# Matmuls of constants in the gaps of TensorE during the first batch's attention

## The chip, the cores and the metric

The kernel runs on one core of one Trainium2 chip. The metric is the device time of one execution in microseconds (us). It was measured three times: 954.39, 951.01 and 953.71 us, median 953.71. One more execution was recorded by the hardware profiler; its page and trace are read below.

The engines are named as in the profile: PE is TensorE's matmul part, PEld its weight loads, DVE VectorE, ACT ScalarE, POOL GpSimd, and SP the engine that issues the DMAs. L182 is line 182 of the kernel before.

## What is computed

A sparse attention with 8 heads over a batch of 8 sequences of 576 positions, and behind it a mixing step over positions and a feed-forward network:

```
scores = (q @ k.T) / sqrt(64)
mask_local   = (rel >= 0) & (rel < 32)                 # heads 0 to 3
mask_strided = (rel >= 0) & (key % 32 == query % 32)   # heads 4 to 7
attn = softmax(where(mask, scores, -1e9))
x = (attn @ v), heads side by side                     # 8 x 576 x 512
h = x.T @ U @ V                                        # 576 -> 32 -> 576, over positions
u = x + h.T
out = u + relu(u @ w_ch1) @ w_ch2                      # 512 -> 2048 -> 512
```

U, V and both weight matrices are 64-bit floats in memory.

## The kernel before

**Stages.** The work has a prefix and nine blocks of 512 positions. The prefix is the attention of batch 0 (`first_attention`, L495), its mixing step, and the first conversions of weights. The nine blocks (the loop at L600) are the two matmuls of the feed-forward network, L431 and L449, each done as three products of high and low parts so that the result has nearly full precision. Into the blocks the loop works the attention and mixing of the next batch.

**The prefix.** Batch 0 has four pairs of heads, in the order 0, 2, 3, 1, started three steps apart (`run_staggered`). One pair goes through this chain:

- `scores` (L140): two bf16 matmuls put the mask into the accumulator (L143), then 36 small f32 matmuls add the scores of 32 queries and up to 64 keys each (L149). In the trace an f32 matmul is two passes, each with its weight load, so a pair's scores are 72 matmul and 72 load records, and 4 for the mask.
- `probabilities` (L154): maximum and subtraction on DVE (L157, L158), exponential on ACT (L161).
- `transposed` (L167): five transpositions on PE (L171), a copy on ACT (L174): 10 records on PE, 5 matmuls and 5 loads.
- `outputs` (L177): 36 small f32 matmuls with the values (L182), 144 records.
- `normalised` (L187): DVE writes the result to `x_loc` or `x_str`.

After the four pairs follow the mixing step (`mix_t`, L319 and L323, and its casts L332 and L333 on ACT), transpositions of the batch's data (L386), the products with V (L359), and then the first matmuls L431 of block 0.

**Weights.** `convert` makes 32-bit floats, split into a high and a low part, out of 32 chunks of 64-bit weights: ACT (L84), DVE (L86, L87, L89), ACT (L112), POOL (L113). The loads of all chunks (`raw`, 512 KB each) are issued on SP right behind the inputs of the attention, so that the queues are full through the prefix. `gate` orders a conversion on ACT behind the last exponential or mixing step.

**What sets the order.** A scheduler reorders the program with a time model of its own (`schedule_with_timeline_sim`), and each engine then runs its own list in order. `tc.issue_after(x)` only tells that scheduler that an instruction is to stand behind `x`. PE's accumulators: `ph` (two buffers) belongs to the first matmul of the network, `acc` and `px` are used by turns in the prefix (`psx2`).

Of the kernel before, what the change touches and what calls it, by code (L numbers as in the profile page):

```python
# [7 lines left out]
F32 = mybir.dt.float32  # L8
F32R = mybir.dt.float32r
BF16 = mybir.dt.bfloat16  # L10
# [6 lines left out]
B, H, S, D = 8, 8, 576, 64  # L17
# [6 lines left out]
NB = B * S // TB  # L24
NSP = 2
LAG = 2
STAGGER = 3
ATT_BUFS = 7
PAIR_ORDER = (0, 2, 3, 1)
# [4 lines left out]
def fused_kernel(ctx, tc, lqk, lv, eqk, ev, sqkv, U, V, wts, masks, eye, out):  # L34
    nc = tc.nc
    const = ctx.enter_context(tc.tile_pool(name="const", bufs=1))
# [5 lines left out]
    ps_h = ctx.enter_context(tc.tile_pool(name="ps_h", bufs=2, space=bass.MemoryType.PSUM))  # L42
    ps_x = ctx.enter_context(tc.tile_pool(name="ps_x", bufs=1, space=bass.MemoryType.PSUM))

    def att(shape, name, dtype=F32):
        return ap_.tile(shape, dtype, name=name, tag="att", bufs=ATT_BUFS)

    banks = {"n": 0, "prefix": True}

    def psx2():  # L50
        banks["n"] += 1
        if banks["prefix"] and banks["n"] % 3:
            return ps_acc.tile([128, 2, 512], F32, name="acc")
        return ps_x.tile([128, 2, 512], F32, name="px")

    last_dma, gate, exps = [None], [], []

    def dma(out, in_):
        last_dma[0] = nc.sync.dma_start(out=out, in_=in_).ins
# [15 lines left out]
    def wtag(i, g, t):  # L75
        return f"w{i}_{g}_{t}"

    def to_f32(raw, p, n, paced=False, after=None):
        rv = raw.bitcast(I32).rearrange("p (n two) -> p n two", two=2)
        lo_w, hi_w = rv[:, 0:n, 0], rv[:, 0:n, 1]  # L80
        cv = att([128, 576], "cv")
        f = cv[0:p, 0:n]
        with tc.issue_after(gate[0]) if paced and gate else nullcontext(), tc.issue_after(after) if after else nullcontext():
            nc.scalar.activation(out=f, in_=hi_w.bitcast(F32), func=AF.Abs, scale=2.0 ** -112)  # L84
        i = cv.bitcast(I32)[0:p, 0:n]
        nc.vector.tensor_scalar(out=i, in0=i, scalar1=3, scalar2=None, op0=ALU.logical_shift_left)  # L86
        nc.vector.scalar_tensor_tensor(out=i, in0=hi_w, scalar=-0x80000000, in1=i,  # L87
                                       op0=ALU.bitwise_and, op1=ALU.bitwise_or)
        nc.vector.scalar_tensor_tensor(out=i, in0=lo_w, scalar=29, in1=i,  # L89
                                       op0=ALU.logical_shift_right, op1=ALU.bitwise_or)  # L90
        return f
# [3 lines left out]
    def load_weights(n):  # L95
        while wl["loaded"] < min(n, len(chunks)):
            k = wl["loaded"]
            c = chunks[k]
            raws[c] = const.tile([128, 512], I64, name="raw%d_%d_%d" % c, tag=wtag(*c))
            with tc.issue_after(last_dma[0]):  # L100
                dma(out=raws[c], in_=wts[k])
            wl["loaded"] += 1

    def convert(n):
        while wl["conv"] < min(n, len(chunks)):
            k = wl["conv"]
            load_weights(k + 1)
            c = chunks[k]
            f = to_f32(raws[c], 128, 512, True, halves_done[-2] if len(halves_done) > 1 else None)
            parts = const.tile([128, 2, 512], F32R, name="w%d_%d_%d" % c, tag=wtag(*c))  # L110
            w_parts[c] = parts
            halves_done.append(nc.scalar.copy(out=parts[:, 0], in_=f).ins)  # L112
            nc.gpsimd.tensor_tensor(out=parts[:, 1], in0=f, in1=parts[:, 0].bitcast(F32), op=ALU.subtract)  # L113
            wl["conv"] += 1
# [7 lines left out]
    def small_loads():  # L122
        dma(out=raw_u, in_=U)
        dma(out=raw_v, in_=V)
# [15 lines left out]
    def scores(kT, qT, mask):  # L140
        sp = psx2()
        for hh in range(2):
            nc.tensor.matmul(sp[:, hh, 0:320], ident_b, mask, start=True, stop=False, skip_group_check=True)  # L143
        for c in range(NCH):
            t, c4 = c // 4, c % 4
            k0 = max(0, 32 * c - 32)
            x0 = 64 * t + (0 if c else 32)
            for hh, rows in enumerate(halves):
                nc.tensor.matmul(sp[32 * c4:32 * c4 + 32, hh, x0:64 * t + 64], qT[rows, 32 * c:32 * c + 32],  # L149
                                 kT[rows, k0:32 * c + 32], start=False, stop=True, skip_group_check=True,  # L150
                                 tile_position=(64 * hh, 32 * c4))
        return sp[:, :, 0:320].rearrange("p h (t x) -> p h t x", x=64)

    def probabilities(sp):  # L154
# [12 lines left out]
    def transposed(s_sb):  # L167
        pp = psx2().rearrange("p a x -> p (a x)")
        for t in range(5):
            n = 128 if t < 4 else 64  # L170
            nc.tensor.transpose(out=pp[:, 128 * t:128 * t + n], in_=s_sb[0:n, t].rearrange("p h x -> p (h x)"),  # L171
                                identity=ident[0:n, 0:n])
        PT = att([128, S], "PT")
        nc.scalar.copy(out=PT, in_=pp[:, 0:S])  # L174
        return PT

    def outputs(PT, vt):  # L177
        op = psx2()
        for c in range(NCH):
            t, c4 = c // 4, c % 4  # L180
            for hh, rows in enumerate(halves):
                nc.tensor.matmul(op[32 * c4:32 * c4 + 32, hh, (D + 1) * t:(D + 1) * t + D + 1], PT[rows, 32 * c:32 * c + 32],  # L182
                                 vt(c)[rows], start=True, stop=True, skip_group_check=True,
                                 tile_position=(64 * hh, 32 * c4))
        return op[:, :, 0:5 * (D + 1)].rearrange("p h (t x) -> p h t x", x=D + 1)

    def normalised(op, pr):  # L187
# [32 lines left out]
    def attention_pair(b, pr, loaded=None):  # L220
# [9 lines left out]
        yield  # L230
        PT = transposed(s_sb)
        yield
        yield
        op = outputs(PT, vt)
        yield
# [122 lines left out]
    def mixed(ps, b, dc, V, s0, s1, start):  # L358
        nc.tensor.matmul(ps, tsts[b][:, 128 * dc:128 * dc + 128], V[:, s0:s1], start=start, stop=True,  # L359
                         skip_group_check=True)  # L360

    def u_local(b, dcs):
        px = psx2()
        for dc in dcs:
            ps = px[:, dc % 2]
            for t in range(4):
                nc.tensor.matmul(ps[:, 128 * t:128 * t + 128], x_loc[:, t, 128 * dc:128 * dc + 128], ident,  # L367
                                 is_transpose=True, start=t == 0, stop=False, skip_group_check=True)
            mixed(ps, b, dc, Vst, 0, TB, False)
        lo, hi = dcs[0] % 2, dcs[-1] % 2 + 1  # L370
        split(b, slice(dcs[0], dcs[-1] + 1), px[:, lo:hi], nc.vector)
# [123 lines left out]
    def first_attention():  # L495
        scratch = [up.tile([128, NDC * TB], F32, name="scr", tag=t) for t in ("uh", "ul")]
        late = [const.tile([128, 9, D + 1], F32, name=f"ve{n}", tag=wtag(n // 4, 3, n % 4)) for n in range(8)]
        loads = {}

        def load(k):  # L500
            pr = PAIR_ORDER[k]
            if k < 3:
                qk = [scratch[j // 3][:, S * (j % 3):S * (j % 3) + S] for j in (2 * k, 2 * k + 1)]
            else:
                qk = [att([128, S], "kT"), att([128, S], "qT")]
            loads[k] = pair_loads(0, pr, (*qk, late[2 * k], late[2 * k + 1]))

        load(0)
        dma(out=masks_sb, in_=masks)
        dma(out=ident, in_=eye)  # L510
        load(1)
        load(2)
        small_loads()
        load(3)
        load_weights(24)
        nc.gpsimd.memset(x_loc[64:128, 4], 0.0)
        nc.gpsimd.memset(x_str[64:128, 4], 0.0)
        pairs = [attention_pair(0, pr, loads[k]) for k, pr in enumerate(PAIR_ORDER)]
        beside = {3: lambda: (small_u(), small_v()), 4: lambda: convert(2)}
        seen = 0  # L520
        steps = run_staggered(pairs, STAGGER)

        def go(n):
            nonlocal seen
            for _ in range(n):
                if next(steps, "end") == "end":
                    return
                if len(exps) > seen:
                    seen = len(exps)
                    beside.get(seen, lambda: None)()  # L530

        go(3 * STAGGER + 8)
        mix_t(0, 1)
        go(2)
        u_strided_early(0, 2)
        go(40)
        mix_t(0, 0)
        u_strided_early(0, 3)
        for dc in range(2):
            u_local(0, (dc,))  # L540
        convert(5)

    first_attention()
# [56 lines left out]
    for n in range(NB):  # L600
        tasks, t = plan(n), 0
        done.clear()
        for fc in range(NFC):
            if n == 0:
                convert(needed(fc))
            gens = [gemm1(n, fc)]
            if len(pend) >= LAG:
                gens.append(gemm2(*pend.pop(0)))
# [91 lines left out]
```

## Time and profile before

| What | Value |
| --- | --- |
| median of 3 timed runs | 953.71 us (951.01 to 954.39) |
| the profiled execution | 954.11 us |
| its span, first to last instruction | 952.3 us |
| PE busy | 917.1 us, 96% of the span |
| DVE, POOL, ACT busy | 536.9, 403.4, 247.3 us |
| moved by DMA | 64.50 MB, mean 68 GB/s |

The page gives averages over the whole span. What matters here is the first 160 us, so the views below are the timeline and the windows of that stretch. In a row of the timeline stand start, duration, engine, line, operation, output and inputs, the count, and in brackets the idle time of the engine just before it with what ended it; "issue" stands for a wait that nothing in the profile explains. The granted clock is the share of TensorE's full speed that its throttle lets through.

### The profile page before, as it was taken

Reading aid. Unit: us, or ns where it says so; the run is one execution under the profiler, and the core shown is the slowest. Engines: PE = TensorE matmul, PEld = TensorE weight load, DVE = VectorE, ACT = ScalarE, POOL = GpSimd, SP = SyncE. Lnnn points to the kernel's source line nnn. Section 1 sums busy time; section 2 is a strip of 40 time slices with the busy share of each in tenths; the row PEclk is TensorE's granted clock in tenths of the full one; section 3 lists DMA queues with packets and bytes.
Section 4 is the critical chain, followed back from the end, with each engine's and each line's share of the span. In section 5 each row is a group of like instructions: output and inputs, shape, how many; then the busy total and the mean of one; then the engine's idle time right before and its main releaser. Section 6 shows DMA issues by size and latency. Waiting matters only on the chain.

```text
span 952.3 us, 16503 instructions
## 1 busy us (share of the span) xinstructions
PE 917.1 (96%) x6896; PEld 725.8 (76%) x6896; DVE 536.9 (56%) x912; ACT 247.3 (26%) x486; POOL 403.4 (42%) x407
## 2 busy tenths in 40 slices
PE   5789898999999999999999999999999999999998
PEld 3557566878787787778778878787778788888886
DVE  4686778548936693659465964597448831112112
ACT  2443345212421142114311341115112521111110
POOL 0142233565639471939185816763575530002000
PEclk9989998999999999999999999999999999999999
DMA  9962202111022101220122003110210020001001
GB/s 338 408 259 67 77 27 75 45 57 52 25 79 71 52 26 56 70 76 5 41 105 77 1 25 119 33 51 26 95 56 26 1 80 15 1 1 45 1 1 44
DMA packets 27098, 64.50 MB, mean 68 GB/s; under 512 B 6768, under 2 KB 7280, under 8 KB 27024
## 3 DMA queue, kind: packets, MB, share of 16 engines
q1 hardware_dynamic: 27024, 63.45, 19.2%
q8 instruction: 54, 0.88, 0.4%
q14 instruction: 20, 0.16, 0.1%
HBM read 52.96 MB, written 10.49 MB: 67 GB/s over the span
## 4 chain that ended last, share of the span: by engine, by line
PE 79%; issue 9%; DVE 4%; POOL 3%; DMA 3%; ACT 0%; SPq 0%; POOLq 0%; DVEq 0%
PE ph L431 37%; PE acc L449 36%; POOL w L113 3%; DVE st L289 2%; DMA raw<-in_wts_dram 2%; PE px L182 1%; PE px L149 1%; PE px L359 1%; PE px L171 1%; DMA ve<-in_ev_dram 1%; PE px L319 1%; PE acc L462 1%; PE px L367 1%; DMA masks_sb<-in_masks_dram 0%; DVE ta L328 0%
## 5 line engine op out<-in xcount | busy, mean ns | idle before, releaser
L431 PE MATMUL ph<-uh,w 128*128 128x512 f32 x1152 | 393.3, 401 | 10.1 <-ACT w L112 5.1
L449 PE MATMUL acc<-gh,w 128*128 128x512 f32 x1136 | 375.4, 392 | 2.2 <-ACT gh L437 1.5
L431 PEld LDWEIGHTS ph<-uh,w 128*128 128x128 f32 x1152 | 217.9, 191 | 62.0 <-ACT w L112 6.7
L449 PEld LDWEIGHTS acc<-gh,w 128*128 128x128 f32 x1136 | 212.7, 188 | 49.0 <-ACT gh L437 2.3
L438 DVE SCALAR_TENSOR_TENSOR gl<-ph,gh 128x512 fp32r<-128x512 f32 x144 | 99.0, 689 | 239.6 <-ACT gh L437 239.0
L431 PE MATMUL ph<-ul,w 128*128 128x512 f32 x576 | 228.7, 398 | 0.0
L449 PE MATMUL acc<-gl,w 128*128 128x512 f32 x568 | 222.4, 392 | 0.0
L261 POOL TENSOR_TENSOR tmp<-st 128x576 f32<-128x576 f32 (+6 forms) x162 | 166.2, 1070 | 88.5 <-DMA st<-in_sqkv_dram 45.4
L437 ACT ACTIVATE gh<-ph 128x512 fp32r<-128x512 f32 x144 | 85.7, 597 | 365.2 <-PE ph L431 341.3
L287 POOL TENSOR_TENSOR tmp<-st,s_st 128x448 f32<-128x448 f32 (+7 forms) x162 | 135.5, 875 | 59.1 <-DVE s_st L280 59.1
L289 DVE TENSOR_REDUCE st<-tmp 128x64 f32<-128x64 f32 (+8 forms) x162 | 133.6, 882 | 1.2 <-POOL tmp L287 0.9
L431 PEld LDWEIGHTS ph<-ul,w 128*128 128x128 f32 x576 | 109.9, 191 | 23.5 <-DVE ul L351 0.6
L449 PEld LDWEIGHTS acc<-gl,w 128*128 128x128 f32 x568 | 106.8, 188 | 22.9 <-issue 0.4
L263 DVE TENSOR_REDUCE s_st<-tmp 128x9 f32<-128x576 f32 (+6 forms) x162 | 87.9, 566 | 44.3 <-POOL tmp L261 44.1
L113 POOL TENSOR_TENSOR w<-cv,w 128x512 fp32r<-128x512 f32 x32 | 43.6, 1369 | 99.2 <-ACT w L112 92.7
L479 POOL TENSOR_TENSOR o<-o,uh 128x512 f32<-128x512 f32 x32 | 40.7, 1297 | 92.8 <-DVE o L478 92.8
L351 POOL TENSOR_TENSOR ul<-st,uh 128x1024 fp32r<-128x1024 f32 x6 | 14.4, 2399 | 103.4 <-ACT uh L350 103.4
L304 ACT COPY x_str<-st 32x256 f32<-32x256 f32 x96 | 38.8, 404 | 36.2 <-DVE st L289 35.0
L87 DVE SCALAR_TENSOR_TENSOR cv<-raw,cv 128x512 int32<-128x512 int32 x32 | 28.4, 892 | 0.4
L112 ACT CAST w<-cv 128x512 fp32r<-128x512 f32 x32 | 19.7, 620 | 31.2 <-DVE cv L89 26.4
L89 DVE SCALAR_TENSOR_TENSOR cv<-raw,cv 128x512 int32<-128x512 int32 x32 | 27.4, 862 | 0.4
L161 ACT ACTIVATE s_sb<-s_sb 128x640 f32<-128x640 f32 x20 | 14.8, 740 | 49.2 <-DVE s_sb L158 49.1
(117 smaller groups left out, 504.4 us busy)
## 6 DMA issues: line engine op xcount, KB each, us to landing
raw<-in_wts_dram SPq DMA_DIRECT2D x32, 512.0 KB, 10.2
st<-in_sqkv_dram SPq DMA_DIRECT2D x18, 576.0 KB, 4.9
out_dram<-o SPq DMA_DIRECT2D x35, 256.0 KB, 2.0
vt<-in_lv_dram SPq DMA_DIRECT2D x14, 585.0 KB, 3.8
kT<-in_lqk_dram SPq DMA_DIRECT2D x15, 288.0 KB, 2.7
qT<-in_lqk_dram SPq DMA_DIRECT2D x15, 288.0 KB, 3.1
ve<-in_lv_dram SPq DMA_DIRECT2D x4, 292.5 KB, 6.0
ve<-in_ev_dram SPq DMA_DIRECT2D x4, 292.5 KB, 5.5
```

Of the source, the lines that this page charges most:

```text
L87: nc.vector.scalar_tensor_tensor(out=i, in0=hi_w, scalar=-0x80000000, in1=i, op0=ALU.bitwise_and, op1=ALU.bitwise_or)
L113: nc.gpsimd.tensor_tensor(out=parts[:, 1], in0=f, in1=parts[:, 0].bitcast(F32), op=ALU.subtract)
L261: nc.gpsimd.tensor_tensor(out=tmp[:, 0:n], in0=sk[:, j0:j0 + n], in1=sq[:, i:i + 1].broadcast_to([128, n, D]), op=ALU.mult)
L263: late.append(lambda tmp=tmp, n=n, i=i, j0=j0: nc.vector.tensor_reduce(out=s_st[:, i, j0:j0 + n], in_=tmp[:, 0:n], axis=AX.X, op=ALU.add))
L287: nc.gpsimd.tensor_tensor(out=tv, in0=sv[:, 0:i + 1, d0:d0 + step], in1=s_st[:, i, 0:i + 1].broadcast_to([128, i + 1, step]), op=ALU.mult)
L289: late.append(lambda tv=tv, i=i, d0=d0, step=step: nc.vector.tensor_reduce(out=sq[:, i, d0:d0 + step], in_=tv.rearrange("p j d -> p d j"), ...
L304: nc.scalar.copy(out=xh[32 * i4:32 * i4 + 32, 0:4], in_=oh[:, i4:16:4])
L431: nc.tensor.matmul(ph, w_parts[0, g, dc][:, part, fs], ut[:, dc, :], start=(k == 0 and i == 0), stop=(k == NDC - 1 and i == 2))
L437: gate[:] = [nc.scalar.activation(out=gh, in_=ph, func=AF.Relu).ins]
L438: nc.vector.scalar_tensor_tensor(out=gl, in0=ph, scalar=0.0, in1=gh.bitcast(F32), op0=ALU.max, op1=ALU.subtract)
L449: nc.tensor.matmul(accs[n][m // 2][:, m % 2], w_parts[1, g, f][:, part, ms], gt, start=(fc == 0 and i == 0), stop=(fc == NFC - 1 and i == 2))
L479: nc.gpsimd.tensor_tensor(out=o, in0=o, in1=uh[:, m].bitcast(F32), op=ALU.add)
```

## The change

A constant tile `warm_w` (128 x 128, bf16, all ones) is made by a memset on POOL. `fill` issues matmuls of that tile with itself into a `ph` buffer; nobody reads the results. There are 80 at the very start, and 20 for each of twelve spots: the last matmul of `scores`, `transposed` and `outputs` of each of the four pairs. The fills of the spots are issued in the program behind `u_local` and ahead of the last conversions, each to stand behind its spot; the scheduler chooses where.

```
+FIRST_FILL, FILL = 80, 20
...
+    warm_w = const.tile([128, 128], BF16, name="warm_w")
+    spots = []
+
+    def spot(matmul):
+        if banks["prefix"]:
+            spots.append(matmul.ins)
+
+    def fill(after, n):
+        ps = ps_h.tile([128, 512], F32, name="ph")
+        for _ in range(n):
+            with tc.issue_after(after) if after is not None else nullcontext():
+                nc.tensor.matmul(ps[:, 0:128], warm_w, warm_w[:, 0:128], start=True, stop=True)
...
# in scores, transposed and outputs: the last matmul of the loop is kept
-                nc.tensor.matmul(sp[...], ...)
+                m = nc.tensor.matmul(sp[...], ...)
+        spot(m)
...
# in first_attention
+        nc.gpsimd.memset(warm_w, 1.0)
+        fill(None, FIRST_FILL)
         load(0)
         dma(out=masks_sb, in_=masks)
...
         for dc in range(2):
             u_local(0, (dc,))
+        for m in spots:
+            fill(m, FILL)
         convert(5)
```

On PE the scheduler put the 240 fills of the spots into seven runs: 26 behind the second scores, 34 behind the first transposition, 34 behind the second, 69 behind the third, 42 behind the fourth, 35 behind the first mixing step and its transposition; together 240. The order of the other matmuls of the prefix stays as it was. In the changed kernel the lines have other numbers: scores are L156 and L162, transpositions L185, outputs L197, the mixing step L335 and L339, its transposition L402, a fill L69.

The first place is PE between the second scores and the first outputs. Before (`s_sb` holds the probabilities, `PT` their transposition, `ve` the values):

```order
L143 MATMUL acc<-masks_sb 128x320
L149 MATMUL acc<-scr 32x32 x2
L149 MATMUL acc<-scr 32x64 x34
L171 MATMUL px<-ident,s_sb 128x128 x4
L171 MATMUL px<-ident,s_sb 128x64
L182 MATMUL acc<-ve_90,PT 32x65 x18
L182 MATMUL acc<-ve_91,PT 32x65 x18
```

The same place of the changed kernel, from the last of the 26 fills to the first of the 34 (each fill is a weight load and a matmul):

```order
L69 LDWEIGHTS warm_w
L69 MATMUL ph<-warm_w 128x128
L185 MATMUL px<-ident,s_sb 128x128 x4
L185 MATMUL px<-ident,s_sb 128x64
L69 LDWEIGHTS warm_w
L69 MATMUL ph<-warm_w 128x128
```

The transposition now stands between two runs of fills, with 52 instructions ahead of it and 68 behind it that were not there.

The second place is PE from the last outputs to the mixing step (`x_str` and `x_loc` are the attention's results, `U_sb` is U). Before:

```order
L182 MATMUL px<-ve_96,PT 32x65 x18
L182 MATMUL px<-ve_97,PT 32x65 x18
L319 MATMUL acc<-x_str,U_sb 32x256 x4
L323 MATMUL acc<-x_str,U_sb 32x64 x4
L386 MATMUL acc<-ident,x_str 128x128 x4
L386 MATMUL acc<-ident,x_str 128x64
L319 MATMUL px<-x_loc,U_sb 32x256 x4
```

In the changed kernel, from the last of the 42 fills to the first of the 35:

```order
L69 MATMUL ph<-warm_w 128x128
L197 MATMUL px<-ve_97,PT 32x65 x18
L197 MATMUL px<-ve_98,PT 32x65 x18
L335 MATMUL acc<-x_str,U_sb 32x256 x4
L339 MATMUL acc<-x_str,U_sb 32x64 x4
L402 MATMUL acc<-ident,x_str 128x128 x4
L402 MATMUL acc<-ident,x_str 128x64
L69 LDWEIGHTS warm_w
L69 MATMUL ph<-warm_w 128x128
```

84 instructions stand ahead of the last outputs, and 70 between the two halves of the mixing step. On DVE and ACT a few neighbours change places, and in block 0 some matmuls of L449 stand earlier against those of L431; POOL has the one memset more, ahead of all others, and SP's list is the same.

More of the change, by code (lines that the diff above doesn't have):

```diff
@@ L148, in scores @@
             for hh, rows in enumerate(halves):
-                nc.tensor.matmul(sp[32 * c4:32 * c4 + 32, hh, x0:64 * t + 64], qT[rows, 32 * c:32 * c + 32],
+                m = nc.tensor.matmul(sp[32 * c4:32 * c4 + 32, hh, x0:64 * t + 64], qT[rows, 32 * c:32 * c + 32],
                                  kT[rows, k0:32 * c + 32], start=False, stop=True, skip_group_check=True,
                                  tile_position=(64 * hh, 32 * c4))
+        spot(m)
         return sp[:, :, 0:320].rearrange("p h (t x) -> p h t x", x=64)
@@ L170, in transposed @@
             n = 128 if t < 4 else 64
-            nc.tensor.transpose(out=pp[:, 128 * t:128 * t + n], in_=s_sb[0:n, t].rearrange("p h x -> p (h x)"),
+            m = nc.tensor.transpose(out=pp[:, 128 * t:128 * t + n], in_=s_sb[0:n, t].rearrange("p h x -> p (h x)"),
                                 identity=ident[0:n, 0:n])
+        spot(m)
         PT = att([128, S], "PT")
@@ L181, in outputs @@
             for hh, rows in enumerate(halves):
-                nc.tensor.matmul(op[32 * c4:32 * c4 + 32, hh, (D + 1) * t:(D + 1) * t + D + 1], PT[rows, 32 * c:32 * c + 32],
+                m = nc.tensor.matmul(op[32 * c4:32 * c4 + 32, hh, (D + 1) * t:(D + 1) * t + D + 1], PT[rows, 32 * c:32 * c + 32],
                                  vt(c)[rows], start=True, stop=True, skip_group_check=True,
                                  tile_position=(64 * hh, 32 * c4))
+        spot(m)
         return op[:, :, 0:5 * (D + 1)].rearrange("p h (t x) -> p h t x", x=D + 1)
```

## The prediction

> **What bounds the kernel now.** I read the page first, then the idle time by stage, then the PE timeline of the stage that the change touches.
>
> ```profile
> PE 917.1 (96%) x6896; PEld 725.8 (76%) x6896; DVE 536.9 (56%) x912; ACT 247.3 (26%) x486; POOL 403.4 (42%) x407
> q8 instruction: 54, 0.88, 0.4%
> 7.39:41.77 34.38, 26.39 (x650) 17.33 (x650) 21.55 (x55) 12.14 (x21) 4.07 (x3) 1.00 1.03 398
> 46.90:60.00 13.10, 8.90 (x34) 5.44 (x33) 12.90 (x18) 7.29 (x14) 5.39 (x4) 0.89 1.03 409
> 160.00:952.30 792.30, 787.43 (x5273) 632.60 (x5272) 428.03 (x710) 181.52 (x371) 361.43 (x370) 1.00 0.14 45
> ```
>
> The second row is PE's instruction queue: packets, MB, share. The last three rows are windows: stretch, length, busy time of PE, PEld, DVE, ACT and POOL, granted clock, DMA share, GB/s. From 160 us on PE is busy 787.43 of 792.30 us, and the change adds nothing there: what it does is decided by when the dense part can begin. Between the first scores at 7.39 and the first dense matmul at 41.77 PE is idle for 34.38 - 26.39 = 7.99 us, and all 16 DMA engines are full (1.03, 398 GB/s of weights and inputs).
>
> Which wait ends last there? The timeline, with PE's own pauses in brackets:
>
> ```profile
> 9.93 1.31 PE L149 MATMUL acc<-scr 64*32 64x32 f32 x72
> 15.31 0.18 PEld L182 LDWEIGHTS acc<-ve,PT 64*32 64x32 f32 x3 [0.21 <-issue]
> 21.75 0.43 PEld L182 LDWEIGHTS acc<-ve,PT 64*32 64x32 f32 x28 [1.35 <-issue]
> 21.75 0.68 PE L182 MATMUL acc<-ve,PT 64*32 64x65 f32 x28 [1.11 <-issue]
> 22.35 0.13 PEld L143 LDWEIGHTS <-masks_sb 128*128 128x128 bf16 x2 [0.17 <-DVE cv L89]
> 22.36 0.72 PE L143 MATMUL acc<-masks_sb 128*128 128x320 bf16 x2
> 23.00 1.07 PEld L149 LDWEIGHTS acc<-kT,qT 64*32 64x32 f32 x72 [0.52 <-issue]
> 23.00 1.31 PE L149 MATMUL acc<-kT,qT 64*32 64x32 f32 x72
> 24.24 0.71 PEld L171 LDWEIGHTS px<-ident,s_sb 128*128 128x128 f32 x4 [0.17 <-issue]
> 24.24 1.41 PE L171 MATMUL px<-ident,s_sb 128*128 128x128 f32 x5
> 25.28 0.18 PEld L171 LDWEIGHTS px<-ident,s_sb 64*128 64x128 f32 x1 [0.33 <-issue]
> 26.43 0.40 PEld L182 LDWEIGHTS acc<-ve,PT 64*32 64x32 f32 x20 [0.97 <-ACT PT L174]
> 26.43 0.64 PE L182 MATMUL acc<-ve,PT 64*32 64x65 f32 x19 [0.78 <-ACT PT L174]
> 28.12 1.10 PE L182 MATMUL acc<-ve,PT 64*32 64x65 f32 x53 [1.05 <-issue]
> 34.32 0.42 PE L182 MATMUL px<-ve,PT 64*32 64x65 f32 x3 [0.40 <-issue]
> ```
>
> PE stops for "issue", that is for no engine, in the middle of four of its output batches (L182): at 15.31, 21.75, 28.12 and 34.32. The steps are 6.44, 6.37 and 6.20 us, on average 6.34. Count the instructions from 21.75 to 28.12: 28+28, 2+2, 72+72, 5+5, 20+19 loads and matmuls make 253. The page's instruction queue q8 moved 54 packets (0.88 MB) for 2 x 6896 PE instructions, 255 to a packet. So each pause falls where one packet of PE's program ends and the next has to be there. The DMA view of 19.10 to 21.75, and of the quiet stretches on both sides of 41.4, has the packets:
>
> ```profile
> q1 hardware_dynamic: 291, 1.06, 100.4%
> q8 instruction: 1, 0.02, 2.5%
> ...
> q14 instruction: 1, 0.01, 0.3%
> ...
> q8 instruction: 1, 0.02, 2.7%
> ```
>
> One q8 packet comes just before the pause at 21.75 ends. Between 34.33 and 41.40 there is none (q14 belongs to another engine), and the next comes in 41.40 to 44.00: up to 7 us after the block at 34.32 began. So I read this stage as **bound by the fetch of PE's instructions**: beside full data queues a new block of some 255 instructions is there every 6.34 us at best, and a faster PE would only wait longer.
>
> A skill rule stands against this: the Trainium skill, "Runtime: NRT & Kernel Launch", Instruction fetch mechanics, says that the program comes in blocks of 256 instructions and that the cost of a block's border is mostly hidden. The trace agrees on the block and not on the cost. By the rule the added instructions would cost only their own time, which is the first rival below.
>
> **The change, part by part.** It adds 320 bf16 matmuls of 128x128, each with its weight load: 640 PE instructions, 80 pairs ahead of the first scores and 240 in seven runs (26, 34, 34, 69, 42, 35; and 80 makes the first). Nothing is removed. POOL gets one memset first. For one pair the trace has no row; the nearest are these:
>
> ```profile
> 0.73 0.31 POOL L516 MEMSET x_loc<- 64x256 f32 x1 [0.29 <-POOLq L688]
> 43.49 1.05 PE L431 MATMUL ph<-uh,w 128*128 128x512 f32 x2
> 44.34 0.63 PE L431 MATMUL ph<-ul,w 128*128 128x512 f32 x1
> 66.45 0.61 PE L431 MATMUL ph<-uh,w 128*128 128x512 f32 x2
> 66.90 0.39 PE L431 MATMUL ph<-ul,w 128*128 128x512 f32 x1
> 7.39 0.13 PEld L143 LDWEIGHTS <-masks_sb 128*128 128x128 bf16 x2 [7.39 <-DMA masks_sb<-in_masks_dram]
> ```
>
> Two dense matmuls of 512 columns take 0.85 us at 43.49 (slow PE) and 0.45 us at 66.45 (fast PE), so 128 columns take 0.107 or 0.057 us. The load, 0.13 / 2 = 0.065, lies beside the matmul before it; were it in the way, a pair would take up to 0.17. I take 0.107 and 0.057, since the dense stream is the like case. **The first 80 pairs** start at about 1.05 (0.73 and a memset like x_loc's 0.31) and last 4.6 to 8.6 us: they end between 5.6 and 9.7. The masks land at 7.39, so I let the scores begin at 8.0.
>
> **The fetch** is the large term. Count instructions from the first score: a pair's scores are 148, a transposition 10, an output batch 144. Before, blocks began at counts 445, 696, 949 and 1203, all inside outputs. The borders stay near these counts, but the new program has 160 fills first, and more between. In it count 445 lies at the end of the second scores, 700 in the first outputs, 953 at the second, 1207 in the fourth scores, 1460 in the third outputs and 1714 in the fourth: **six block starts where there were four**. The border at 189 stood in the second scores (row 9.93) at about 10.2, and the block at 445 came 15.31 - 10.2 = 5.1 us later. Now count 189 is in the first scores, at about 8.2; so 445 comes at 13.4, and five steps later, at 13.4 + 5 x 6.34 = 45.1, the last part of the fourth outputs can run. What follows it before the first dense matmul is seen here:
>
> ```profile
> 34.68 1.08 PE L319 MATMUL acc<-x_str,U_sb 128*32 128x256 f32 x8
> 41.77 1.22 PE L431 MATMUL ph<-uh,w 128*128 128x512 f32 x2 [0.48 <-ACT uh L350]
> ```
>
> From 34.68 to 41.77 is 7.1 us; to it come 0.6 for the 66 instructions left of the outputs and 2.8 for the run of 35 fills (between 35 x 0.057 = 2.0 and 35 x 0.107 = 3.7), and 0.7 goes if PE is fast half of the time. The first dense matmul then starts at 45.1 + 0.6 + 7.1 + 2.8 - 0.7 = 54.9, not at 41.77: **13.1 us later**.
>
> The other fills (205 in the gaps) I cost at nothing, because the fetch covers them: where PE is fast, a block with its fills has at most some 5.6 us of work against 6.34. If PE is slow that cover is gone (the second rival).
>
> **Is it made good later?** The rows that carry the delay on:
>
> ```profile
> 45.64 0.40 ACT L333 CAST tst<-ta 32x256 fp32r<-32x256 f32 x1
> 46.06 1.24 ACT L84 ACTIVATE cv<-raw 128x512 f32<-128x512 f32 x2
> 50.13 0.73 PE L431 MATMUL ph<-uh,w 128*128 128x512 f32 x2 [1.45 <-ACT w L112]
> 57.10:64.00 6.90, 5.82 (x14) 4.62 (x15) 6.70 (x10) 2.70 (x5) 2.97 (x2) 0.51 0.79 297
> ```
>
> The next weight conversion (L84) follows the casts of the mixing step (L333) on ACT, and PE waits for converted weights at 50.13; DVE is busy 12.90 of 13.10 us from 46.90. ACT, DVE, POOL and SP keep their work in nearly the same order, so this stage moves as a whole and I carry all of the 13.1 us. A fast PE in 41.77 to 46.90 would reach the same wait for weights sooner: nothing. The slow spell at 57.10 to 64.00 (granted clock 0.51) follows idle time; if it doesn't return, up to 2.9 us of PE's 5.82 are won, and if there is one more as much is lost. I take zero.
>
> Sum against the profiled execution: 954.11 (span 952.3 and 1.8 around it) + 13.1 = 967.2. The median of the three timed runs is 953.71, 0.4 lower; I say **967.0**.
>
> **The rivals.** *1. A fast PE, and the fetch hides: not slower.* For it: PE was slow throughout this stage, as like operations show, early and late:
>
> ```profile
> L171 PE MATMUL px<-ident,s_sb 128*128 128x128 f32 x12 | 3.3, 434 | 0.7 <-ACT s_sb L161 0.7
> L182 PE MATMUL acc<-ve,PT 64*32 64x65 f32 x216 | 5.1, 312 | 4.4 <-ACT PT L174 2.2 <-issue 2.2
> ...
> L171 PE MATMUL px<-ident,s_sb 128*128 128x128 f32 x12 | 1.9, 277 | 1.0 <-ACT s_sb L161 1.0
> L182 PE MATMUL px<-vt,PT 64*32 64x65 f32 x216 | 2.9, 225 | 0.8 <-ACT PT L174 0.8
> ```
>
> 434 against 277 ns and 312 against 225: about 0.3 of the 26.39 us, 8 us, could go. (The granted clock of 1.00 in that window can't be the whole record, since like operations take a third less later; the durations decide.) With the 7.99 idle that is room for 16, and the 240 fills take 240 x 0.057 = 13.7: 2 us earlier at best, 951.5. The Trainium skill, "TensorE: Matmul & The Clock Gate", Part 1, speaks for this rival: PE runs at half clock until some 3.4 us of steady matmuls, and falls back after a like idle window. The trace agrees with it in 57.10 to 64.00: in the 13.10 us from 46.90 PE was idle for 4.2. Against the rival: the four pauses. The point: solving 13.4 + 5s + 9.8 = 41.77 gives s = 3.7; if a block comes every 3.7 us or faster, the change isn't slower.
>
> *2. The fills don't keep PE fast: it does not do what it says.* The pauses leave PE without work for microseconds, and it may fall back each time. Then blocks overrun the fetch: the block of S2's end, 26 and 34 fills, transposes and outputs takes 8.7 us (+2.4), that with 69 fills 9.6 (+3.3), the other two about 0.7 each, the last run of 35 0.9 more, the lost 0.7, and a start at 9.6 in place of 8.0: some 10 us, at 977.
>
> *3. The fetch is quicker than 6.34,* as the first 5.1 us step was: 5 x 1.2 = 6 less, 961.
>
> **How the numbers follow.** Forecast 0.60, first rival 0.12, second 0.15, third 0.13. The range takes the forecast, the third with 2.9 us for the lost slow spell (961 - 3 = 958) and the second (977, and one late packet as after 34.32): 958 to 978. A measurement of this kernel can tell about 0.5% (4.8 us) from no change. Faster by more than that would need over twice the best that the first rival has: 0.03; same 0.12 with the milder end of the third; slower 0.85.
>
> **What would show it.** Right: "issue" pauses of PE 250 to 256 instructions apart, about 6.3 us from one to the next, six of them and some within scores; the first dense matmul near 55; the dense stage after it as long as before. The fills at 0.057 to 0.107 us. Wrong: no pauses, a first dense matmul at 42 or earlier, or a q8 packet that comes at once after a border in spite of full queues.

## The result

The changed kernel takes 965.28 us (median of 4 runs, 963.94 to 966.35), the kernel before 952.36 (4 runs beside them): 12.9 us more, a ratio of 1.0141 with a 95% interval of 1.011 to 1.0171. The profiled execution has 966.35 us against 954.11, its span 964.3 against 952.3.

The page of the changed kernel, PE and its instruction queue (packets, MB, share), and the windows of the same two stages as before (stretch, length, busy time of PE, PEld, DVE, ACT, POOL, granted clock, DMA share, GB/s):

```profile
PE 929.4 (96%) x7216; PEld 742.8 (77%) x7216; DVE 539.4 (56%) x912; ACT 247.6 (26%) x486; POOL 403.9 (42%) x408
q8 instruction: 56, 0.92, 0.4%
```

```profile
7.92:55.03 47.11, 35.75 (x893) 30.03 (x891) 21.29 (x55) 12.21 (x21) 3.72 (x3) 0.86 1.03 400
172.00:964.30 792.30, 787.41 (x5276) 632.75 (x5275) 428.84 (x710) 181.82 (x372) 361.61 (x370) 1.00 0.14 45
```

The last 792.30 us hold 787.41 us of PE work, before 787.43: the dense part is untouched. The stage between the first scores and the first dense matmul takes 47.11 us in place of 34.38. PE now does run fast for most of it: five transpositions take 0.86 us at 42.81, and 1.41 us in the kernel before. (The granted clock is 0.86 here, with the slow stretches counted in. The 1.00 that is recorded for the stage before doesn't fit the durations: in e7 below the same five take 1.41 us, and there the record says 0.50.) And PE is still idle for 47.11 - 35.75 = 11.4 us, more than the 8.0 before, with 9.4 us of busy time added. The timeline of PE says where (the rows that are used below):

```profile
1.00 7.08 PE L69 MATMUL ph<-warm_w 128*128 128x128 bf16 x80 [1.00 <-POOL warm_w L524]
7.92 0.43 PE L156 MATMUL acc<-masks_sb 128*128 128x320 bf16 x2
13.92 0.43 PE L162 MATMUL acc<-scr 64*32 64x64 f32 x6 [3.56 <-issue]
14.28 2.95 PE L69 MATMUL ph<-warm_w 128*128 128x128 bf16 x26
18.32 2.77 PE L69 MATMUL ph<-warm_w 128*128 128x128 bf16 x34
27.69 0.27 PE L69 MATMUL ph<-warm_w 128*128 128x128 bf16 x2 [1.79 <-issue]
33.89 0.64 PE L162 MATMUL acc<-kT,qT 64*32 64x64 f32 x21 [3.97 <-issue]
35.80 6.15 PE L69 MATMUL ph<-warm_w 128*128 128x128 bf16 x69
43.60 2.52 PE L69 MATMUL ph<-warm_w 128*128 128x128 bf16 x42
48.00 0.46 PE L197 MATMUL px<-ve,PT 64*32 64x65 f32 x32 [1.28 <-issue]
49.86 2.13 PE L69 MATMUL ph<-warm_w 128*128 128x128 bf16 x35
55.03 0.73 PE L447 MATMUL ph<-uh,w 128*128 128x512 f32 x2 [0.75 <-ACT uh L366]
```

Four pauses for "issue", 3.56 + 1.79 + 3.97 + 1.28 = 10.6 us, nearly all of the idle time. They now stand in the scores too, and the one that ends at 27.69 stands inside a run of fills. That row matters: a fill reads one constant tile and writes a buffer that nobody reads, so PE can't have been waiting there for data or for another engine. The first dense matmul starts at 55.03 in place of 41.77.

### The profile page after: what moved, and what is told of

It reads as the page before. It is cut to its first block, busy times and chain, and to the rows that moved or that the text cites. A ratio compares the mean times of both kernels' runs of the same rounds, so it can differ in the third digit from the quotient of the medians.

```text
span 964.3 us, 17141 instructions
## 1 busy us (share of the span) xinstructions
PE 929.4 (96%) x7216; PEld 742.8 (77%) x7216; DVE 539.4 (56%) x912; ACT 247.6 (26%) x486; POOL 403.9 (42%) x408
## 4 chain that ended last, share of the span: by engine, by line
PE 82%; issue 6%; DVE 5%; DMA 4%; POOL 2%; ACT 1%; SPq 0%; DVEq 0%; POOLq 0%; ACTq 0%
PE ph L447 37%; PE acc L465 37%; DMA raw<-in_wts_dram 3%; POOL w L126 2%; DVE st L305 2%; PE px L197 1%; PE px L162 1%; PE px L375 1%; PE px L185 1%; DMA ve<-in_ev_dram 1%; PE px L335 1%; PE acc L478 1%; PE px L383 1%; DMA masks_sb<-in_masks_dram 1%; DVE cv L100 0%
## 5 line engine op out<-in xcount | busy, mean ns | idle before, releaser
L102 DVE SCALAR_TENSOR_TENSOR cv<-raw,cv 128x512 int32<-128x512 int32 x32 | 29.2, 914 | 0.4
L100 DVE SCALAR_TENSOR_TENSOR cv<-raw,cv 128x512 int32<-128x512 int32 x32 | 28.6, 898 | 0.5
```

## The experiments

Theory A is that of the prediction: beside full data queues a block of 256 PE instructions comes about every 6.3 us, and the added instructions cost block starts. Theory B: the fills stand in the way by their own time. Theory C: a fast PE pays. Ten kernels were run, each beside the kernel before on the same chip. The first dense matmul is read from one traced execution of each. e2 and e10 begin alike and yet start their scores at 7.23 and 8.08 us, so about 0.9 us of such a figure can be chance. An excerpt leaves out rows where it has "...".

| Run | Added PE instructions | First dense matmul | Time, us | Before beside it | Ratio (95%) |
| --- | --- | --- | --- | --- | --- |
| before | 0 | 41.77 | 952.36 | | |
| after | 640 | 55.03 | 965.28 | 952.36 | 1.0141 (1.011 to 1.0171) |
| e1_wide | 256 | 47.50 | 957.21 | 953.01 | 1.0053 (1.0032 to 1.0074) |
| e2_small | 640 | 52.32 | 964.50, 1 run | 953.01 | |
| e3_late_before | 0 | 40.09 | 954.86 | 953.01 | 1.0024 (1.0013 to 1.0035) |
| e4_late_after | 640 | 48.61 | 961.35 | 953.01 | 1.0091 (1.0075 to 1.0107) |
| e5_held | 0 | 40.41 | 953.63 | 953.17 | 1.0004 (0.9988 to 1.002) |
| e6_held_after | 640 | 45.31 | 958.07, 1 run | 953.17 | |
| e7_first | 160 | 43.31 | 955.84, 1 run | 953.17 | |
| e8_gaps | 480 | 49.70 | 962.96, 1 run | 953.17 | |
| e9_held_wide | 256 | 44.98 | 954.27 | 953.08 | 1.002 (1.000 to 1.004) |
| e10_small_double | 1120 | 63.65 | 967.46, 1 run | 953.08 | |

### All the instructions, little of the time (e2), and twice as many (e10)

```
-                nc.tensor.matmul(ps[:, 0:128], warm_w, warm_w[:, 0:128], start=True, stop=True)
+                nc.tensor.matmul(ps[0:32, 0:32], warm_w[:, 0:32], warm_w[:, 0:32], start=True, stop=True)
```

and for e10 besides

```
-FIRST_FILL, FILL = 80, 20
+FIRST_FILL, FILL = 80, 40
```

> The same 320 fills with 32 columns of weights and 32 columns moved: all 640 instructions, but about 0.03 us each, some 7 us in place of 19 in the gaps, and too little work to make PE fast. Theory A: still bound by block starts, first dense matmul at 50 or later, with pauses adding up to over 10 us. Theory B: at most 43 to 44, since most of the fills' time is gone.

PE of e2, from its timeline:

```profile
13.26 0.43 PE L162 MATMUL acc<-scr 64*32 64x64 f32 x6 [2.32 <-issue]
...
19.78 0.45 PE L197 MATMUL acc<-ve,PT 64*32 64x65 f32 x10 [1.98 <-issue]
...
26.07 0.37 PE L69 MATMUL ph<-warm_w 128*32 128x32 bf16 x7 [1.47 <-issue]
...
32.32 0.44 PE L162 MATMUL acc<-kT,qT 64*32 64x64 f32 x26 [3.06 <-issue]
...
38.41 0.44 PE L197 MATMUL acc<-ve,PT 64*32 64x65 f32 x26 [2.11 <-issue]
38.78 0.86 PE L185 MATMUL acc<-ident,s_sb 128*128 128x128 f32 x5
39.56 1.88 PE L69 MATMUL ph<-warm_w 128*32 128x32 bf16 x64
41.90 0.74 PE L197 MATMUL px<-ve,PT 64*32 64x65 f32 x33 [0.46 <-ACT PT L189]
44.54 0.93 PE L197 MATMUL px<-ve,PT 64*32 64x65 f32 x39 [1.89 <-issue]
```

Six pauses, 12.8 us in all, at steps of 6.52, 6.29, 6.25, 6.09 and 6.13 us. Between the last two stand 26 + 5 + 64 + 33 = 128 matmuls, each with its load: 256 instructions, to the one. The fills have lost more than half of their time (64 in 1.88 us, 0.029 each, against 42 in 2.52 in the changed kernel, 0.060 each), and the first dense matmul comes at 52.32, 10.6 us late; B had at most 44.

> The small fills (32 by 32) with 40 in place of 20 for each spot: 480 more instructions than with the small fills before, nearly all ahead of the first dense matmul, and some 7 us more of PE time. Theory A: two further block starts of 6.1 to 6.3 us each, then the queues run empty; first dense matmul at 60 to 65 in place of 52.3. A rival by which the 10 us of the small fills were a fixed cost of any fills: 53 to 57.

The end of that stage in e10, and then a row of ACT from e10 and from e2:

```profile
45.33 0.72 PE L197 MATMUL px<-ve,PT 64*32 64x65 f32 x45 [2.08 <-issue]
...
51.52 0.35 PE L69 MATMUL ph<-warm_w 128*32 128x32 bf16 x8 [1.20 <-issue]
...
57.91 0.25 PE L69 MATMUL ph<-warm_w 128*32 128x32 bf16 x4 [1.35 <-issue]
```

```profile
59.58 1.23 ACT L97 ACTIVATE cv<-raw 128x512 f32<-128x512 f32 x2
```

```profile
56.61 1.24 ACT L97 ACTIVATE cv<-raw 128x512 f32<-128x512 f32 x2
```

The 480 more instructions bring two more pauses, 6.19 and 6.39 us on, both among fills, and the first dense matmul comes at 63.65, within A's 60 to 65; a fixed cost of any fills would have left it at 53 to 57. So the start of the dense part moves with the instructions and in steps of a block. The whole does not follow it here: it is 3.0 us over e2, and not 11. The scheduler moved a part of the later matmuls ahead of the first dense one, and ACT's next weight conversion, which PE needs soon after, starts at 59.58 in place of 56.61: those 3.0 us are what the whole lost. That this conversion is what decides is a reading of the two traces, and was not tested.

### The same columns in fewer instructions (e1)

```
-FIRST_FILL, FILL = 80, 20
+FIRST_FILL, FILL = 32, 8
-    warm_w = const.tile([128, 128], BF16, name="warm_w")
+    warm_w = const.tile([128, 320], BF16, name="warm_w")
-                nc.tensor.matmul(ps[:, 0:128], warm_w, warm_w[:, 0:128], start=True, stop=True)
+                nc.tensor.matmul(ps[:, 0:320], warm_w[:, 0:128], warm_w, start=True, stop=True)
```

> The same columns of constants in 128 fills of 320 columns in place of 320 fills of 128: 256 added PE instructions, not 640, and about the same busy time of PE. Theory A (fetch of PE's program, one block of 256 instructions per 6.3 us): one more block start than in the kernel before and none further, first dense matmul at 45 to 46 us in place of 55.0 (before 41.8); pauses of PE 256 instructions apart remain. Theory B (the fills stand in the way of the real matmuls by their own time): first dense matmul still at 53 to 55. Theory C (a fast PE pays once the fetch hides it): 38 to 40, only if there are no pauses.

The first dense matmul starts at 47.50, 5.7 us late in place of 13.3, and the whole is 4.2 us over the kernel before in place of 12.9: about three fifths of the loss go with three fifths of the instructions, though PE moves as many columns as in the changed kernel. (The trace is of an execution of 961.05 us, the slowest of five from 956.63 up.) The start is 1.5 us above A's figure. Of the five block starts by the count, three show a pause, of 0.91, 4.32 and 0.73 us. Behind the long one stand fills on a slow PE:

```profile
21.88 0.43 PE L162 MATMUL acc<-scr 64*32 64x64 f32 x6 [4.32 <-issue]
...
23.59 4.45 PE L69 MATMUL ph<-warm_w 128*128 128x320 bf16 x16
27.97 1.09 PE L197 MATMUL acc<-ve,PT 64*32 64x65 f32 x72
```

16 fills take 4.45 us there, and 2.35 at 37.18 us, where PE is fast. So the pause costs twice: it lets PE fall back to half speed, and the fills that were to keep it fast then run slowly.

### The queues emptied (e3 and e5), and with the fills (e4 and e6)

The late kernels hold back the weights after the fifth chunk until the last pair's attention is written. The held ones, whose edit is shown here, hold back all of them, in two steps, and load the last ones only six chunks ahead of their conversion. A copy of two numbers out of the finished attention into the chunk's buffer makes the load wait.

```
+            if held:
+                nc.gpsimd.tensor_copy(out=raws[c].bitcast(F32)[0:1, 0:2], in_=held.pop())
             with tc.issue_after(last_dma[0]):
                 dma(out=raws[c], in_=wts[k])
...
-            load_weights(k + 1)
+            load_weights(k + (1 if banks["prefix"] else 7))
...
-        load_weights(24)
...
-        go(3 * STAGGER + 8)
+        go(10)
+        held[:] = [x_loc[0:1, 0, 0:2]]
+        load_weights(2)
+        go(3 * STAGGER - 2)
...
         go(40)
+        held[:] = [x_loc[0:1, 0, 128:130]]
+        load_weights(14)
...
-    load_weights(32)
+    load_weights(16)
```

> The kernel before, with the weight chunks after the fifth held back until the last pair's attention is written (one small copy on POOL ahead of the sixth chunk's load), so that the DMA queues run empty in the attention. Nothing is changed on PE. Theory A: the four pauses of PE in the outputs go, and the first dense matmul comes 2 to 3 us earlier, at 39 to 40. Theory B and a rival by which the pauses are no fetch: first dense matmul at 41.8 as before. The whole time follows, if the later weights still land before they are converted.

> The kernel before, with the weights held in two steps: the first two chunks until the first pair's attention is written, the others until the last pair's, and from the 17th chunk on each load six chunks ahead of its conversion, so that the loads of the next batch's attention stand ahead of the last weights. Nothing is changed on PE. Theory A: the inputs alone fill the queues to about 14 us; no pause of over 0.5 us after that, first dense matmul at 37 to 39 (before 41.8, with only the later weights held 40.1), and the whole some 3 us shorter, at 949 to 951, as PE no longer waits for the next batch's q as it did with all weights held. If the pauses are no fetch: 41.8 and no gain.

PE of e3, then the outputs and the first dense matmul of e5:

```profile
21.92 0.68 PE L184 MATMUL acc<-ve,PT 64*32 64x65 f32 x28 [2.04 <-issue]
...
26.61 1.38 PE L184 MATMUL acc<-ve,PT 64*32 64x65 f32 x72 [0.78 <-ACT PT L176]
...
76.57 0.91 PE L151 MATMUL px<-kT,qT 64*32 64x32 f32 x72 [2.85 <-DMA qT<-in_eqk_dram]
```

```profile
20.26 1.37 PE L184 MATMUL acc<-ve,PT 64*32 64x65 f32 x72 [0.73 <-ACT PT L176]
...
26.94 1.22 PE L184 MATMUL acc<-ve,PT 64*32 64x65 f32 x72 [2.45 <-ACT PT L176]
...
33.24 1.37 PE L184 MATMUL px<-ve,PT 64*32 64x65 f32 x72 [2.57 <-ACT PT L176]
...
40.41 0.73 PE L433 MATMUL ph<-uh,w 128*128 128x512 f32 x2 [0.77 <-ACT uh L352]
```

In e3 the pause at 21.92 is still there, while the queues are full (DMA share 1.02 from 14 to 24 us); the later outputs run in one piece (share 0.22 from 24 to 34 us). In e5 that pause has gone as well. PE's order in this stage is the same in all three, so the pauses belong to the full queues. But the first dense matmul comes only 1.7 and 1.4 us earlier, less than A's 2 to 3 and, for e5, 3 to 5. In part that is a late start (e5's scores begin at 7.97, before at 7.39), and what is late next is the copy PT on ACT, 2.45 and 2.57 us of waiting in e5. And neither is faster as a whole. In e3 PE waits at 76.57 for the next batch's q, which queued behind the weights; e5 has no such wait, and is level with the kernel before all the same, where A had 949 to 951. Its traced execution has a span of 951.5 against 952.3, but the runs of either kernel lie 4.5 to 5.4 us apart, and a gain of 1 us would not show among them.

> The changed kernel with the same held-back weights: all 640 added instructions and all the fills' time, but no full queues. Theory A: most of the 13 us goes; without the pauses (11 us in the changed kernel) the first dense matmul comes at 42 to 44. Theory B: it stays at 53 to 55.

> The changed kernel with the weights held in the same two steps: all 640 instructions, all the fills' time, and no full queues from about 14 us. Theory A: no pauses after that; what is left of the 13 us is the fills' own time, first dense matmul at 41 to 44, that is 3 to 6 us behind the kernel with held weights and no fills. Theory B (the fills' own time makes the 13 us): 12 us or more behind it.

The pauses of e4, and then of e6:

```profile
14.14 0.31 PE L164 MATMUL acc<-scr 64*32 64x64 f32 x6 [3.85 <-issue]
...
26.42 0.27 PE L69 MATMUL ph<-warm_w 128*128 128x128 bf16 x2 [1.33 <-issue]
...
30.15 0.42 PE L164 MATMUL acc<-kT,qT 64*32 64x64 f32 x21 [1.50 <-issue]
```

```profile
13.86 0.31 PE L164 MATMUL acc<-scr 64*32 64x64 f32 x6 [3.82 <-issue]
...
28.47 0.42 PE L164 MATMUL acc<-kT,qT 64*32 64x64 f32 x21 [1.68 <-issue]
```

e4's first dense matmul comes at 48.61, between A's 42 to 44 and B's 53 to 55: three pauses are left, 6.7 us in all, and A had none. e6's comes at 45.31, 4.9 us behind e5; A had 3 to 6, B 12 or more.

e5 and e6 are the pair that weighs the parts. With full queues the fills put the first dense matmul off by 55.03 - 41.77 = 13.3 us; with held weights, and the same fills, by 45.31 - 40.41 = 4.9. So some 8.4 us of the 13.3 are the meeting of the added instructions with full queues, counting the stretches in which PE is slow behind a pause. What is left is not the fills' own time alone: the first pause of e6, 3.82 us, falls while the inputs of the attention themselves fill the queues (DMA share 1.04 from 7.4 to 14 us), and holding the weights can't remove it. A said there would be no pause later, which was wrong: one of 1.68 us remains.

### The two halves of the change (e7, e8)

Only the constants differ: 80 and 0, then 0 and 20.

> Only the 80 fills at the start, none in the gaps; weights as in the kernel before. Theory A: the 160 instructions push each border 160 back, so that the first wait for a block falls in the second scores (13 to 14 us) and PE waits again at 20, 26 and 33, now ahead of the last outputs: first dense matmul at 44 to 45. Theory B: the fills end about when the masks land; 42.3 at most.

> Only the 240 fills in the gaps, none at the start. The scheduler puts about 200 of them ahead of the first dense matmul. Theory A: two block starts more than in the kernel before, first dense matmul at 49 to 52, pauses 6.3 us apart. Theory B: 53 to 55, since nearly all of the fills' time stays.

PE of e7, then of e8:

```profile
13.61 0.43 PE L162 MATMUL acc<-scr 64*32 64x64 f32 x6 [3.02 <-issue]
...
20.20 0.67 PE L162 MATMUL acc<-scr 64*32 64x64 f32 x30 [1.26 <-issue]
...
26.62 1.10 PE L162 MATMUL acc<-kT,qT 64*32 64x64 f32 x55 [1.26 <-issue]
...
32.68 0.43 PE L197 MATMUL acc<-ve,PT 64*32 64x65 f32 x5 [1.55 <-issue]
```

```profile
22.41 1.03 PE L69 MATMUL ph<-warm_w 128*128 128x128 bf16 x12 [3.12 <-issue]
...
28.65 0.46 PE L162 MATMUL acc<-kT,qT 64*32 64x64 f32 x31 [2.45 <-issue]
...
40.91 0.46 PE L197 MATMUL px<-ve,PT 64*32 64x65 f32 x31 [1.32 <-issue]
```

With the 80 fills at the start alone, the pauses move by 160 instructions: to 13.6, 20.2, 26.6 and 32.7, as forecast, the first three now in scores. The first dense matmul is 1.5 us late (43.31 against 41.77). About half of that is the fills' own time: they run until 8.30, and the scores begin at 8.14 in place of 7.39. A's 44 to 45 was a little high, B's limit of 42.3 too low. The gaps alone cost 7.9 us (A: 49 to 52, measured 49.70). Together the halves give 9.5 of the 13.3 us. By the count, e8 crosses six block borders in this stage, as many as the changed kernel; but in the changed kernel 7.0 us of work are left behind the last, in e8 some 2, since its last border stands in the last run of fills. That fits the 3.8 us that are missing, and was not tested.

### Is a fast PE worth anything? (e9)

> Held weights together with the wide fills (128 fills of 320 columns, 256 instructions): PE fast and hardly any wait for its program. Theory C (a fast PE pays once the fetch hides it): first dense matmul at 38 to 39, ahead of the 40.4 with held weights and no fills, and the whole some 2 us shorter than before. Rival D: with PE out of the way the chain over DVE and ACT (PE waits 2.5 us each for the copies ahead of the third and the fourth outputs there) sets this stage, and fills only add their own time where they outlast a gap: 41 to 43, no gain over the kernel before.

It has the wide fills of e1 and the held weights of e5. The first dense matmul comes at 44.98, 4.6 us behind e5 without fills; the whole is 1.0 to 1.004 times the kernel before. D has the sign, and its 41 to 43 missed what is left of the pauses:

```profile
20.61 0.43 PE L164 MATMUL acc<-scr 64*32 64x64 f32 x6 [2.95 <-issue]
...
22.32 4.45 PE L69 MATMUL ph<-warm_w 128*128 128x320 bf16 x16
```

Theory C's forecast failed, but its condition wasn't met: the fetch was not hidden, and PE fell back to half speed behind that pause. Where no pause is left, the stage with a fast PE is the shorter one. These are the windows from the fourth pair's masks to the first dense matmul, of e9 and then of e5:

```profile
27.75:44.98 17.23, 16.48 (x334) 11.51 (x330) 12.59 (x38) 7.85 (x14) 4.21 (x4) 1.00 0.39 136
```

```profile
21.56:40.41 18.85, 11.97 (x277) 8.04 (x274) 14.65 (x43) 8.13 (x15) 4.21 (x4) 0.73 0.37 129
```

e9 takes 1.6 us less there, with 56 fills more, at a granted clock of 1.00 against 0.73. It had lost 6.2 us before that point (27.75 against 21.56). A fast PE would explain the 1.6 us; so would DVE and ACT, which had 6.2 us more to get ahead there, and no run tells the two apart. No version that I ran beats the kernel before.

## Why the prediction was right

The forecast was 967.0, the measured time 965.28, and the mechanism held: beside full queues PE waits for blocks of its program, which come about every 6.3 us where it waits. The closeness of the number is in part luck, as the terms show. (The sum itself gives 967.2 - 0.4 = 966.8, not 967.0.)

**Fills at the start.** Forecast to begin at 1.05 and to let the scores begin at 8.0; they began at 1.00, took 7.08 us, and the scores began at 7.92.

**The block starts.** Forecast: six, from 13.4 to 45.1, 6.34 apart. The first is at 13.92, the last at 48.00, so a step was 34.08 / 5 = 6.8. Only four of the six show a pause. The other two, by the count of 256, lie in the first and the third outputs, at about 21.8 and 42.3, that is 7.9 and 8.4 us after the one before; there the fills outlasted the fetch: 26 and 34 fills took 2.95 and 2.77 us (0.113 and 0.081 each), 69 took 6.15 (0.089). The steps behind them were the shorter for it, 5.9 and 5.7. So the term "the other fills I cost at nothing, because the fetch covers them" was too low by some 2.4 us (5 x 0.48), and 0.5 comes of the first block, 13.92 against 13.4: the second rival, PE falling back to half speed in the pauses, was partly there.

**From the last block to the first dense matmul.** Forecast 9.8 us (0.6 + 7.1 + 2.8 - 0.7), measured 55.03 - 48.00 = 7.0, since PE was fast all through: the 35 fills took 2.13 in place of 2.8, and most of the rest is the 7.1 - 0.7, where I had allowed for a slow half. This error and the one before it, 2.8 early and 2.9 late, cancel by luck: the 13.1 us came out as 13.3, better than the working deserves.

**Carried to the end.** All of it, I said; the span grew by 12.0. From the first dense matmul to the dense part's start (160.0 before, 172.0 after) it is 117.0 us in place of 118.2, so 1.3 us came back. The slow spell that I had at 57.10 moved to another place and is shorter:

```profile
64.20:67.60 3.40, 3.40 (x10) 2.33 (x10) 3.33 (x4) 1.47 (x3) 2.07 (x2) 0.50 0.47 112
```

PE is busy in it for 3.40 us in place of 5.82, and about half of such time is lost to the slow clock: 1.2 us less. (Two more slow spells stand later, in either kernel.) That would do for the 1.3 us, but it was not tested.

**The first rival** lost on its own condition: blocks would have had to come every 3.7 us. PE did become fast (granted 0.86 over the stage; 42 fills in 2.52 us, 0.060 each): without the 18.75 us of the fills its operations take 35.75 - 18.75 = 17.0 us of the stage, and 26.39 before. And yet the stage did not become shorter, since the fills and 10.6 us of waiting for the program take more than that. The fills' time alone does not explain it: in e2 they take 7.8 us, and the first dense matmul is still 10.6 us late. The Trainium skill, "TensorE: Matmul & The Clock Gate", Part 1, has PE fall back to half speed after an idle window of about 3.4 us. In the changed kernel the pauses of 3.56 and 3.97 us are followed by slow operations and those of 1.79 and 1.28 us are not, which agrees. But e9's pause of 2.95 us was enough, and so was the stretch ahead of 57.10 in the kernel before, where no pause of PE is over 1.45 us; for that stretch the prediction called the trace in agreement too easily.

## What to carry to other kernels

Before adding work to an engine because it is idle or slow, find what it idles for: an idle time put down to "issue" that recurs at a fixed count of instructions, 256 here, points to the fetch of its own program, and then each added instruction costs a share of a block, however little it computes. Instructions that must be added should be few and wide (12.9 us with 640 of them, 4.2 with 256 that move the same columns). And a stage that loads its inputs at full rate is the worst place for them: a block came every 6.1 to 6.5 us there, and 3.75 us after the one before where the queues were idle.

## What was not expected of the hardware

A block takes time even when the queues are empty. This window of e4 lies between two block starts, 127 matmuls with their loads apart (the last three figures are granted clock, DMA share and GB/s):

```profile
26.40:30.15 3.75, 2.23 (x127) 1.62 (x127) 3.46 (x11) 0.66 (x1) 0.00 (x0) 1.00 0.02 4
```

The DMA share is 0.02, and PE still paused for 1.50 us: a block came 3.75 us after the one before, against 6.1 to 6.5 in e2's full queues. The one packet of PE's program in this window moves at 27.5, 1.1 us after the border, and PE goes on 2.6 us later. So with idle queues a border is hidden only where PE takes longer than some 3.7 us for 256 instructions. The attention's small matmuls don't (72 of them with their loads, 144 instructions, take 0.92 us on a fast PE); the dense part does (787.41 us for 5276 matmuls with their loads, about 19 us for 256 instructions). The Trainium skill, "Runtime: NRT & Kernel Launch", Instruction fetch mechanics, has the cost of a border mostly hidden. The dense part agrees with that, the attention does not.
